# Pooling adds cut into pieces of 256 columns, and the low half of q subtracted on VectorE

## The chip, the cores and the metric

The kernel runs on one core of a Trainium2 chip. The metric is the device time of one launch in microseconds. A core has five engines that each work through a queue of their own in order: TensorE (PE in the profile; PEld are its weight loads), VectorE (DVE), ScalarE (ACT), GpSimd (POOL) and SyncE (SP, which here only issues DMAs). They wait for one another through semaphores.

## The reference

An attention over pooled keys, and then a layer of experts of which each row visits one:

```python
# q (4, 12288, 128), kv (4, 384, 32, 128), w_sr (128, 128)
kv_pool = kv.reshape(B, H // 4, 4, W // 4, 4, C).mean(axis=(2, 4))   # 96 x 8 = 768 keys a batch
k = v = kv_pool.reshape(B, -1, C) @ w_sr
a = softmax(q @ k.T / sqrt(C));  x = a @ v                           # 49152 rows of 128
# experts: E = 8, w1 (8, 128, 1024), w2 (8, 1024, 128)
do_compute = x @ w_skip > 0
e_idx = argmax(x @ w_gate);  gate_w = its softmax probability
y = gate_w * (relu(x @ w1[e_idx]) @ w2[e_idx])
out = where(do_compute, x + y, x)
```

## The kernel before

The program has two stages. The first, up to about 1180 us of the profile, does the attention and the routing; the second runs the experts in a loop over groups of rows. Both changes are in the first.

**Tiles and steps.** The first stage is a loop over `t`, one step for each tile of 128 query rows: 96 tiles a batch, four batches, 384 tiles, and `tb` is the tile's number in its batch. Twelve tiles make a row of work (`RT`), four make a group (`GT`). The order of the instructions is written out by hand (`manual_schedule`): each engine's queue holds its instructions in the order in which the program issues them. A step issues, for different tiles, in this order:

- `scores(t)` on TensorE: six matmuls of q with k. q and k are each held as a high and a low part, so that one product takes three matmuls (L578, L579, L580); the last uses q's low part.
- `attend(t - 6)` and `p_transpose(t - 1)` on TensorE (L641, L616).
- `row_max(t)` on VectorE (L586), once per tile, and `row_exp(t)` on ScalarE (L591), which waits for it. There are two PSUM buffers for scores, so that `scores(t + 2)` waits for `row_exp(t)`.
- `early_a` on ScalarE: q's high part for a later group (`q_hi`, L566). `early_g`: q's low part, `q_lo` = q - `q_hi` (L567), for 512 columns, once every four steps, in the steps that leave 2 when divided by 4. `q_split` puts both there for the group that is used six tiles later.
- `split_v` (L624), `early_v` (L649, L651) and `p_lo(t - 1)` (L599) on VectorE. L599 reads two operands from SBUF; L624 reads one from PSUM and one from SBUF. `p_lo` then issues the DMA that transposes the probabilities (on the SP queue).
- `load_q` and `load_kv`: DMA loads on the SP queue.
- `run_jobs`: the routing of finished rows, a generator that is advanced step by step. Its element operations are on VectorE and GpSimd (L688 to L770). At its end it scatters the 12 tiles of a row to their experts' lists with 12 indirect DMAs, which GpSimd issues (`scatter_rows`, L184), two per step in the steps that leave 6 to 11 when divided by 12. The next row's first routing operations (L692 to L708) come behind the first two of them, and L721 behind the tenth.
- the pooling of the next batch's keys and values: `pool_kv(b + 1, k)` for six chunks k. A chunk is a tile `kvt` of 128 partitions and 16 x 128 columns; GpSimd halves it by adds of 1024, 512 and 256 columns in place (L437), and a last add of 128 columns writes `pooled` (L439). Chunk k's loads are spread over the steps before; four steps after the last one it is put on the list `pools`, and in the next step with `tb % 12 == 11` all four adds of one chunk are issued at once. The first batch's chunks are pooled before the loop, mostly on VectorE; from `tb` = 84 on the pooled chunks are transposed and multiplied for the next batch.

Batches two, three and four are pooled during the loop, so 18 chunks are; the last 96 tiles pool nothing.

Of the kernel before, what the change touches and what calls it, by code (L numbers as in the profile page):

```python
# [9 lines left out]
F32 = mybir.dt.float32  # L10
# [5 lines left out]
ALU = mybir.AluOpType  # L16
# [4 lines left out]
RT = 12  # L21
# [3 lines left out]
def kernel(  # L25
# [11 lines left out]
    nc = tc.nc  # L37
    NR, C, RT, P = q.shape
# [7 lines left out]
    E, _, FF = w1.shape  # L46
# [22 lines left out]
    PSL = 11  # L69
# [97 lines left out]
    op = ctx.enter_context(tc.tile_pool(name="op", bufs=2))  # L167
# [199 lines left out]
    with ExitStack() as p1:  # L367
# [40 lines left out]
        def load_kv(b, k, rs=range(R)):  # L408
            if rs[0] == 0:
                KVT[b, k] = kvp.tile([P, R, R * C], F32, name="kvt")  # L410
            src = kv[b, k * HG * R:(k + 1) * HG * R].rearrange("(i r) (g w) c -> r i g (w c)", r=R, w=R)
            for r in rs:
                nc.sync.dma_start(KVT[b, k][:, r, :], src[r])

        def pooled_out(b, k):
            if k == 0:
                pooled[b] = kprep.tile([P, KC, C], F32, name="pooled")
            return KVT.pop((b, k)), pooled[b][:, k, :]
# [12 lines left out]
        def pool_kv(b, k):  # L431
            t, o = pooled_out(b, k)
            f = t.rearrange("p r x -> p (r x)")
            n = R * R * C
            while n > 2 * C:
                n //= 2
                nc.gpsimd.tensor_tensor(out=f[:, 0:n], in0=f[:, 0:n], in1=f[:, n:2 * n], op=ALU.add)  # L437
                yield
            nc.gpsimd.tensor_tensor(out=o, in0=f[:, 0:C], in1=f[:, C:2 * C], op=ALU.add)  # L439

        HK = NK // 2
# [95 lines left out]
        def prep_kv(b):  # L537
            for f in (kv_transpose, k_matmul):
                for h in range(2):
                    f(b, h * HC, (h + 1) * HC)  # L540
                    yield
            yield from prep_v(b)
# [6 lines left out]
        def load_q(g):  # L549
            r, o = divmod(g, RG)  # L550
            q_sb[g] = qp.tile([P, GW], F32, name="q_sb")
            nc.sync.dma_start(q_sb[g], q[r][:, o * GT:(o + 1) * GT, :].rearrange("c t p -> c (t p)"))

        early_a, early_g, late_a, early_v, jobs = [], [], [], [], []
# [3 lines left out]
        def run_late(q):  # L558
            while q:
                q.pop(0)()  # L560

        def q_split(g):
            q_g = q_sb.pop(g)
            hi = qt.tile([P, GW], F32R, name="q_hi")
            lo = qt.tile([P, GW], F32R, name="q_lo")
            early_a.append(lambda: nc.scalar.copy(hi, q_g))  # L566
            early_g.append(lambda: nc.gpsimd.tensor_tensor(out=lo, in0=q_g, in1=hi.bitcast(F32), op=ALU.subtract))  # L567
            qT[g] = (hi, lo)

        def scores(t):  # L570
            g, j = divmod(t, GT)
            k_hi, k_lo = KV[t // TPB][0:2]
            q_hi, q_lo = (x[:, j * P:(j + 1) * P] for x in qT[g])
            s = ps_s.tile([P, 2, 512], F32, name="s_ps")
            S_PS[t] = s
            for h in range(2):
                sl = slice(h * HK, (h + 1) * HK)
                nc.tensor.matmul(s[:, h, :HK], q_hi, k_hi[:, sl], start=True, stop=False)  # L578
                nc.tensor.matmul(s[:, h, :HK], q_hi, k_lo[:, sl], start=False, stop=False)  # L579
                nc.tensor.matmul(s[:, h, :HK], q_lo, k_hi[:, sl], start=False, stop=True)  # L580
# [3 lines left out]
        def row_max(t):  # L584
            NM[t] = small.tile([P, 1], F32, name="nm")
            nc.vector.tensor_reduce(out=NM[t], in_=S_PS[t][:, :, :HK], axis=AX.XY, op=ALU.max, negate=True)  # L586

        def row_exp(t):
            g, j = divmod(t, GT)
            P_SB[t] = pp.tile([P, 2, HK], F32, name="p_sb")  # L590
            nc.scalar.activation(out=P_SB[t], in_=S_PS.pop(t)[:, :, :HK], func=AF.Exp, bias=NM.pop(t))  # L591

        def p_hi(t):
            P16[t] = hl.tile([P, 2, KD * P], F16, name="p16")
            nc.scalar.activation(out=P16[t][:, 0, :], in_=p_flat(t)[:, 0:KD * P], func=AF.Copy, scale=2.0 ** PEXP)  # L595

        def p_lo(t):
            p16 = P16.pop(t)
            nc.vector.scalar_tensor_tensor(out=p16[:, 1, :], in0=p_flat(t)[:, 0:KD * P], scalar=2.0 ** PEXP,  # L599
                                           in1=p16[:, 0, :], op0=ALU.mult, op1=ALU.subtract)  # L600
            P_SB.pop(t)
            PT[t] = ptp.tile([P, 2 * KD, P], F16, name="pt")
            nc.sync.dma_start_transpose(PT[t], p16.rearrange("p a x -> p (a x)"))

        def p_flat(t):
            return P_SB[t].rearrange("p h x -> p (h x)")
# [3 lines left out]
        def p_transpose(t):  # L610
            g, j = divmod(t, PP)
            if j == 0:
                PTP[g] = acc_ps()
            p = p_flat(t)
            for i in range(KP):
                nc.tensor.transpose(PTP[g][:, (j * KP + i) * P:(j * KP + i + 1) * P],  # L616
                                    p[:, (KD + i) * P:(KD + i + 1) * P], ident)
            if j < PP - 1:
                return
            ps = PTP[g][:, 0:PP * KP * P]  # L620
            hl_t = ptq.tile([P, 2, PP * KP * P], F16, name="ptq")
            PTQ[g] = hl_t.rearrange("p a (j k x) -> p a j k x", j=PP, x=P)
            next_a.append(lambda: nc.scalar.activation(out=hl_t[:, 0, :], in_=ps, func=AF.Copy, scale=2.0 ** PEXP))
            next_v.append(lambda: nc.vector.scalar_tensor_tensor(  # L624
                out=hl_t[:, 1, :], in0=ps, scalar=2.0 ** PEXP, in1=hl_t[:, 0, :], op0=ALU.mult, op1=ALU.subtract))
# [268 lines left out]
        pools = []  # L894
# [14 lines left out]
        while t < NTILE + LAG - 1 or jobs:  # L909
            t += 1  # L910
            b, tb = divmod(t, TPB)
            live = t < NTILE
            for now, nxt in ((split_a, next_a), (split_v, next_v), (late_a, next_l)):
                now.extend(nxt)
                nxt.clear()
            if live:
                scores(t)
            if 0 <= t - LAG < NTILE:
                attend(t - LAG)
            if 0 <= t - 1 < NTILE:  # L920
                p_transpose(t - 1)
            if live:
                row_max(t)
            run_late(early_a)
            run_late(split_a)
            if 0 <= t - 1 < NTILE:
                p_hi(t - 1)
            run_late(late_a)
            if live:
                row_exp(t)  # L930
            run_late(early_g)
            run_late(split_v)
            run_late(early_v)
            if 0 <= t - 1 < NTILE:
                p_lo(t - 1)
            if live:
                if t % GT == 0 and t // GT + RG < NGRP:
                    load_q(t // GT + RG)
                if b + 1 < B:
                    for k, r in KV_T.get(tb, ()):  # L940
                        load_kv(b + 1, k, [r])
                if b + 1 < B and tb == PREP_T:
                    preps.append(prep_kv(b + 1))
                if t in PAD_T:
                    write_pads(*PADS.pop(0))
            first_step(NTILE - t)
            if t == NTILE:
                p_s.close()
                p_kv.close()
                alloc_h(p1.enter_context(tc.tile_pool(name="hp1", bufs=1)))  # L950
                ps_up = p1.enter_context(tc.tile_pool(name="ps_up", bufs=4, space=PSUM))
                alloc["h"] = lambda: ps_up.tile([P, ST], F32, name="up_ps")
            ph = t % GT
            if ph == 1 and t // GT + 2 < NGRP:
                q_split(t // GT + 2)
            ranked = run_jobs(ph)
            if preps and not ranked and (ph in (0, 3) or tb < LAG):
                if next(preps[0], "end") == "end":
                    preps.pop(0)
            if live and b + 1 < B:  # L960
                for k, r in KV_T.get(tb - 4, ()):
                    if r == R - 1:
                        pools.append(pool_kv(b + 1, k))
                if pools and tb % RT == PSL:
                    for _ in pools.pop(0):
                        pass
            for _ in range(2 * (t >= NTILE)):
                next(first)
        for _ in make_table():
# [76 lines left out]
```

## Time and profile before

| | |
|---|---|
| time, median of 3 runs | 2067.53 us (2058.41, 2067.53, 2076.75) |
| profiled execution, its own time | 2057.81 us |
| its span, first to last instruction | 2056.1 us |
| mean granted TensorE clock | 0.949 |
| busy: TensorE, weight loads | 1830.2, 1308.1 us |
| busy: VectorE, ScalarE, GpSimd | 1549.2, 1302.8, 1068.9 us |
| L567 (`q_lo`) on GpSimd | 96 times, 125.9 us |
| L184 scatters of routed rows on GpSimd | 384 times, 385.5 us |
| L586 (`row_max`) on VectorE | 384 times, 363.7 us |

The profile is of one execution. In lines of a timeline the columns are start and duration in us, engine, line, operation, output and inputs with shapes, and in brackets how long the engine stood idle before and what ended that. In lines of groups, after the count: busy us, mean ns of one, idle us before. In lines of stretches: the stretch, its length, each engine's busy us with its number of instructions, then the granted share of the TensorE clock, the busy share of the DMA engines, and GB/s.

### The profile page before, as it was taken

The numbers are of one execution on the slowest core, as the hardware profiler recorded it, in microseconds if no ns is written. First come the engines' busy times: TensorE is split into PE (matmuls) and PEld (weight loads), VectorE is DVE, ScalarE is ACT, GpSimd is POOL, SyncE is SP. The second block draws the span as 40 slices with busy tenths as digits, with TensorE's granted clock in tenths as the row PEclk, the third lists the DMA queues.
The fourth block names the chain that finished last, engine by engine and source line by source line (L and its number), as shares of the span: only waits on it lengthen the run. The fifth ranks groups of instructions, "written<-read, shape, count | busy, mean of one in ns | idle before, by whom it ended". The sixth has DMA issues, their size and how long they took to land. (4 is left out here: it accounts for less than half of the span.)

```text
span 2056.1 us, 42524 instructions
## 1 busy us (share of the span) xinstructions
PE 1830.2 (89%) x13955; PEld 1308.1 (64%) x13955; DVE 1549.2 (75%) x3222; ACT 1302.8 (63%) x2480; POOL 1068.9 (52%) x1296
## 2 busy tenths in 40 slices
PE   4998888989898888898988867999999999999997
PEld 3987878878787787887878733444444444444443
DVE  7987857878686787776867746777777777777776
ACT  3876767767676676766767724656565655555564
POOL 2277674677756768655565753343333333333433
PEclk9999988999999899988999978999999999999999
DMA  7998988889789789878997832433333343333333
GB/s 173 209 193 173 184 165 165 182 157 167 147 161 170 156 177 184 169 164 175 191 185 169 176 73 74 107 98 88 92 88 92 88 103 100 94 90 90 91 89 88
DMA packets 620914, 284.61 MB, mean 138 GB/s; under 512 B 502112, under 2 KB 570848, under 8 KB 620768
## 3 DMA queue, kind: packets, MB, share of 16 engines
q1 hardware_dynamic: 599264, 244.30, 58.3%
q0 software_dynamic: 21504, 38.43, 6.2%
q8 instruction: 83, 1.36, 0.3%
q14 instruction: 63, 0.52, 0.1%
HBM read 90.60 MB, written 78.64 MB: 82 GB/s over the span
## 5 line engine op out<-in xcount | busy, mean ns | idle before, releaser
L184 POOL DMA_INDIRECT out_dram<-o,xin x288 | 299.7, 1040 | 510.7 <-DVE o L293 422.9
L586 DVE TENSOR_REDUCE nm<-s_ps 128x1 f32<-128x768 f32 x384 | 363.7, 947 | 208.7 <-PE s_ps L580 129.8
L270 DVE SCALAR_TENSOR_TENSOR h_lo<-h_ps,h_hi 128x512 f16<-128x512 f32 x544 | 343.1, 685 | 174.1 <-ACT h_hi L269 174.1
L591 ACT ACTIVATE p_sb<-s_ps,nm 128x768 f32<-128x768 f32 x384 | 346.5, 902 | 195.2 <-DVE nm L586 152.9
L184 POOL DMA_INDIRECT scr<-rows,di x384 | 385.5, 1004 | 149.6 <-issue 122.9
L641 PE MATMUL acc_ps<-v_hi,pt 128*128 128x138 f16 x3072 | 339.9, 232 | 90.8 <-DVE ptq L624 36.1
L641 PEld LDWEIGHTS <-pt 128*128 128x128 f16 x4608 | 294.2, 101 | 166.1 <-issue 164.9
L269 ACT ACTIVATE h_hi<-h_ps 128x512 f16<-128x512 f32 x544 | 298.9, 594 | 41.8 <-PE h_ps L268 17.9
L599 DVE SCALAR_TENSOR_TENSOR p<-p_sb,p 128x512 f16<-128x512 f32 x384 | 316.2, 824 | 1.6 <-ACT p L595 1.0
L578 PE MATMUL s_ps<-k_hi,q_hi 128*128 128x384 f32 x768 | 305.1, 397 | 7.6 <-issue 7.6
L641 PE MATMUL acc_ps<-v_lo,pt 128*128 128x138 f16 x1536 | 309.7, 231 | 2.2 <-issue 2.2
L579 PE MATMUL s_ps<-k_lo,q_hi 128*128 128x384 f32 x768 | 268.7, 350 | 4.9 <-issue 4.9
L580 PE MATMUL s_ps<-k_hi,q_lo 128*128 128x384 f32 x768 | 267.6, 348 | 5.7 <-issue 5.7
L595 ACT ACTIVATE p<-p_sb 128x512 f16<-128x512 f32 x384 | 242.0, 630 | 5.5 <-DMA pt<-p 2.2
L266 PE MATMUL h_ps<-xT,w_hi 128*128 128x512 f16 x544 | 206.1, 379 | 24.9 <-issue 24.9
L285 ACT ACTIVATE yT<-y_ps,y_sc 128x512 f32<-128x512 f32 x68 | 46.7, 687 | 276.9 <-PE y_ps L282 217.1
L282 PE MATMUL y_ps<-h_hi,w_hi 128*128 128x512 f16 x544 | 206.2, 379 | 0.0
L282 PE MATMUL y_ps<-h_hi,w_lo 128*128 128x512 f16 x544 | 206.2, 379 | 0.0
L268 PE MATMUL h_ps<-xT,w_lo 128*128 128x512 f16 x544 | 206.1, 379 | 0.0
L267 PE MATMUL h_ps<-xT,w_hi 128*128 128x512 f16 x544 | 206.1, 379 | 0.0
L282 PEld LDWEIGHTS <-w_hi 128*128 128x128 f16 x1152 | 113.4, 98 | 134.7 <-issue 4.5
L567 POOL TENSOR_TENSOR q_lo<-q_sb,q_hi 128x512 fp32r<-128x512 f32 x96 | 125.9, 1312 | 138.0 <-ACT q_hi L566 137.7
(215 smaller groups left out, 3283.7 us busy)
## 6 DMA issues: line engine op xcount, KB each, us to landing
kvt<-in_kv_dram SPq DMA_DIRECT2D x96, 256.0 KB
q_sb<-in_q_dram SPq DMA_DIRECT2D x96, 256.0 KB
out_dram<-rows SPq DMA_DIRECT2D x96, 256.0 KB
xin<-scr SPq DMA_DIRECT2D x75, 264.0 KB, 2.7
w_raw<-in_moe_w_dram SPq DMA_DIRECT2D x38, 512.0 KB, 4.0
scr<-pad SPq DMA_DIRECT2D x32, 264.0 KB
pt<-p SPq DMA_TRANSPOSE x384
scr<-rows,di POOLq DMA_INDIRECT x384
```

The lines of the kernel that those rows point to most:

```text
L184: ins = nc.gpsimd.indirect_dma_start(out=dst, out_offset=bass.IndirectOffsetOnAxis(ap=ids, axis=0), in_=src, in_offset=None, bounds_check= ...
L269: nc.scalar.activation(out=h["hi"][:, c, :], in_=ps, func=AF.Relu)
L270: nc.vector.scalar_tensor_tensor(out=h["lo"][:, c, :], in0=ps, scalar=0.0, in1=h["hi"][:, c, :], op0=ALU.max, op1=ALU.subtract)
L282: nc.tensor.matmul(ps, w[:, c, :], h[x][:, c, :], start=(i == 0), stop=(i == len(terms) - 1))
L578: nc.tensor.matmul(s[:, h, :HK], q_hi, k_hi[:, sl], start=True, stop=False)
L579: nc.tensor.matmul(s[:, h, :HK], q_hi, k_lo[:, sl], start=False, stop=False)
L580: nc.tensor.matmul(s[:, h, :HK], q_lo, k_hi[:, sl], start=False, stop=True)
L586: nc.vector.tensor_reduce(out=NM[t], in_=S_PS[t][:, :, :HK], axis=AX.XY, op=ALU.max, negate=True)
L591: nc.scalar.activation(out=P_SB[t], in_=S_PS.pop(t)[:, :, :HK], func=AF.Exp, bias=NM.pop(t))
L595: nc.scalar.activation(out=P16[t][:, 0, :], in_=p_flat(t)[:, 0:KD * P], func=AF.Copy, scale=2.0 ** PEXP)
L599: nc.vector.scalar_tensor_tensor(out=p16[:, 1, :], in0=p_flat(t)[:, 0:KD * P], scalar=2.0 ** PEXP, in1=p16[:, 0, :], op0=ALU.mult, op1=ALU ...
L641: nc.tensor.matmul(ps[:, j % 2, :], w, v[a][:, k, :], start=(i == 0), stop=(i == len(AVL) - 1))
```

## The change

The subtraction that makes `q_lo` is issued on VectorE in place of GpSimd, and its place in the step moves from behind `row_exp` to behind `p_lo`. The two start-up groups' `q_lo` move to VectorE too.

The pooling's adds of 1024, 512 and 256 columns become four, two and one adds of 256 columns; the last add stays. A step issues one of the eight adds of the chunk at the head of the list (two from `tb` = 74 on), from the step in which the chunk is put on the list, in place of all of them in one step of twelve. Chunks are put on the list at `tb` = 13, 26, 39, 52, 65 and 78.

```diff
             n = R * R * C
+            m = 2 * C
             while n > 2 * C:
                 n //= 2
-                nc.gpsimd.tensor_tensor(out=f[:, 0:n], in0=f[:, 0:n], in1=f[:, n:2 * n], op=ALU.add)
-                yield
+                for c in range(0, n, m):
+                    nc.gpsimd.tensor_tensor(out=f[:, c:c + m], in0=f[:, c:c + m], in1=f[:, n + c:n + c + m], op=ALU.add)
+                    yield
             nc.gpsimd.tensor_tensor(out=o, in0=f[:, 0:C], in1=f[:, C:2 * C], op=ALU.add)
...
-            early_g.append(lambda: nc.gpsimd.tensor_tensor(out=lo, in0=q_g, in1=hi.bitcast(F32), op=ALU.subtract))
+            early_g.append(lambda: nc.vector.tensor_tensor(out=lo, in0=q_g, in1=hi.bitcast(F32), op=ALU.subtract))
...
             if live:
                 row_exp(t)
-            run_late(early_g)
             run_late(split_v)
             run_late(early_v)
             if 0 <= t - 1 < NTILE:
                 p_lo(t - 1)
+            run_late(early_g)
...
-                if pools and tb % RT == PSL:
-                    for _ in pools.pop(0):
-                        pass
+                for _ in range(2 if tb >= 74 else 1):
+                    if pools and next(pools[0], "end") == "end":
+                        pools.pop(0)
```

## The prediction

> **What bounds the kernel now.** I read the busy shares first, then the busy time in chosen stretches, then the count of row maxima (L586, one per query tile) as a clock of tiles, and last the timelines of GpSimd and VectorE.
>
> ```profile
> span 2056.1 us, 42524 instructions
> PE 1830.2 (89%) x13955; PEld 1308.1 (64%) x13955; DVE 1549.2 (75%) x3222; ACT 1302.8 (63%) x2480; POOL 1068.9 (52%) x1296
> ```
>
> No engine is full over the span, so stages decide. The change lives in the attention stage, up to about 1180 us.
>
> ```profile
> core 0: us, PE busy (x) PEld busy (x) DVE busy (x) ACT busy (x) POOL busy (x), PEclk, DMA share, GB/s
> 47.00:117.00 70.00, 69.67 (x762) 65.00 (x763) 64.61 (x116) 61.52 (x113) 25.34 (x34) 1.00 1.04 198
> 354.00:373.00 19.00, 19.00 (x211) 17.71 (x209) 17.78 (x37) 16.50 (x31) 9.62 (x17) 1.00 1.11 192
> 341.00:345.00 4.00, 1.48 (x9) 1.28 (x9) 0.00 (x0) 0.00 (x0) 3.39 (x4) 0.94 1.17 288
> 345.00:352.00 7.00, 5.99 (x38) 5.25 (x38) 4.48 (x8) 4.39 (x8) 5.10 (x6) 0.54 0.38 85
> 770.00:790.00 20.00, 18.13 (x203) 16.63 (x202) 16.31 (x28) 15.96 (x31) 15.17 (x17) 1.00 0.99 215
> ```
>
> In a smooth stretch (354 to 373) TensorE is busy all 19.00 us and VectorE 17.78: TensorE sets the pace and VectorE has 6% left. At 341 to 345 all but GpSimd stand still: VectorE 0.00, TensorE 1.48 of 4; then the granted clock is 0.54 for 7 us. The row maxima give the price:
>
> ```profile
> L586 DVE TENSOR_REDUCE nm<-s_ps x25: 944/952/958, 46.9 to 103.5; 128x1 f32<-128x768 f32 x25
> L586 DVE TENSOR_REDUCE nm<-s_ps x73: 894/949/958, 361.3 to 576.0; 128x1 f32<-128x768 f32 x73
> L586 DVE TENSOR_REDUCE nm<-s_ps x49: 894/957/959, 945.3 to 1087.5; 128x1 f32<-128x768 f32 x49
> L586 DVE TENSOR_REDUCE nm<-s_ps x13: 895/949/958, 760.7 to 792.8; 128x1 f32<-128x768 f32 x13
> ```
>
> Per 12 tiles: 56.6/24 x 12 = 28.3 us before scatters begin, 214.7/72 x 12 = 35.8 with scatters and pooling, 142.2/48 x 12 = 35.5 with scatters and none of the pooling (the last batch), and one odd dozen of 32.1. So pooling itself costs about 0.3 us per dozen tiles, and what comes with the scatters about 7.2. GpSimd around one such place:
>
> ```profile
> 331.39 1.08 POOL L184 DMA_INDIRECT scr<-rows,di  x1 [1.00 <-POOL rows L772]
> 332.78 0.97 POOL L184 DMA_INDIRECT scr<-rows,di  x1 [0.30 <-issue]
> 333.77 0.37 POOL L692 TENSOR_TENSOR d<-lg,mx 128x96 f32<-128x96 f32 x1
> ...
> 336.62 1.07 POOL L184 DMA_INDIRECT scr<-rows,di  x1 [0.52 <-issue]
> 337.99 0.97 POOL L184 DMA_INDIRECT scr<-rows,di  x1 [0.30 <-issue]
> ...
> 343.09 0.97 POOL L184 DMA_INDIRECT scr<-rows,di  x1 [0.30 <-issue]
> 344.06 1.30 POOL L567 TENSOR_TENSOR q_lo<-q_sb,q_hi 128x512 fp32r<-128x512 f32 x1
> 345.53 0.99 POOL L184 DMA_INDIRECT scr<-rows,di  x1 [0.17 <-issue]
> ...
> 347.81 0.62 POOL L721 TENSOR_TENSOR oh_all<-oh,act 128x96 bf16<-128x96 f32 x1
> ...
> 349.93 0.97 POOL L184 DMA_INDIRECT scr<-rows,di  x1 [0.30 <-issue]
> ```
>
> ```profile
> 339.59 0.26 DVE L720 TENSOR_TENSOR oh<-em,mn 128x96 f32<-128x96 f32 x1
> 345.43 0.96 DVE L586 TENSOR_REDUCE nm<-s_ps 128x1 f32<-128x768 f32 x1 [5.59 <-remote]
> ```
>
> Call the 12 scatters of a row s1 to s12. s1 and s2 come in the step whose number leaves 6 when divided by 12 (step 6 below), then two per step to step 11. GpSimd runs behind, so s3 to s8 go out back to back, 1.28 us apart, from 336.62; four scatters in, TensorE stalls, and VectorE waits 5.59 us. q_lo stands behind s8 by program order. Nothing in the trace names what the stalled TensorE lacks; that it comes with scatters in a row is what I use.
>
> **Part 1: q_lo to VectorE.** Prices of like work there, and what an add of 256 columns takes on GpSimd:
>
> ```profile
> L624 DVE SCALAR_TENSOR_TENSOR ptq<-acc_ps,ptq 128x512 f16<-128x512 f32 x140 | 95.2, 680 | 0.0
> L526 DVE TENSOR_TENSOR v_lo<-misc,v_hi 128x411 f16<-128x411 f32 x6 | 3.5, 586 | 2.9 <-ACT v_hi L525 2.9
> L599 DVE SCALAR_TENSOR_TENSOR p<-p_sb,p 128x512 f16<-128x512 f32 x384 | 316.2, 824 | 1.6 <-ACT p L595 1.0
> L567 POOL TENSOR_TENSOR q_lo<-q_sb,q_hi 128x512 fp32r<-128x512 f32 x96 | 125.9, 1312 | 138.0 <-ACT q_hi L566 137.7
> L437 POOL TENSOR_TENSOR kvt<-kvt 128x256 f32<-128x256 f32 x19 | 17.8, 936 | 1.5
> ```
>
> A 512-column subtraction on VectorE is not shown. It lies between 0.59 (411 columns) and the 0.82 mean of L599, the like operation that shares its time with GpSimd; I take 0.68, from L624, of the same width. 96 of them are +65 us of VectorE. GpSimd loses 96 x 1.31, none of it on the path.
>
> Two stand in the start-up, between the k_lo of 31.44 and the k_lo that waits 1.72 us for ScalarE, and are hidden if they take under that:
>
> ```profile
> 31.44 0.41 DVE L465 SCALAR_TENSOR_TENSOR k_lo<-acc_ps,k_hi 128x256 fp32r<-128x256 f32 x1
> 33.57 0.29 DVE L465 SCALAR_TENSOR_TENSOR k_lo<-acc_ps,k_hi 128x128 fp32r<-128x128 f32 x1 [1.72 <-ACT k_hi L464]
> ```
>
> The rest come in steps 2, 6 and 10. About 30 stand in step 10 and lie in the 5.59 us wait; if that wait goes they cost what the others do. Some 64 fall in stretches where VectorE has 1.22 us left in 19 (about 8 tiles, two q_lo, 1.36 us): it goes from 94% to full. Against that, q_lo on GpSimd no longer blocks L599:
>
> ```profile
> 499.29 1.28 POOL L567 TENSOR_TENSOR q_lo<-q_sb,q_hi 128x512 fp32r<-128x512 f32 x1
> 499.92 1.20 DVE L599 SCALAR_TENSOR_TENSOR p<-p_sb,p 128x512 f16<-128x512 f32 x1
> 502.08 0.68 DVE L599 SCALAR_TENSOR_TENSOR p<-p_sb,p 128x512 f16<-128x512 f32 x1
> ...
> 162.75 5.22 POOL L437 TENSOR_TENSOR kvt<-kvt 128x1024 f32<-128x1024 f32 x3
> ...
> 163.70 2.00 DVE L599 SCALAR_TENSOR_TENSOR p<-p_sb,p 128x512 f16<-128x512 f32 x1
> ```
>
> L599 takes 0.68 alone and 1.20 where it starts under q_lo: up to 0.52 in this pair. Not every q_lo meets one; I take 0.2. So VectorE gains 0.48 per q_lo against 0.6 spare; since the spare time isn't where the work falls, I charge 0.2 us each on the path: 64 x 0.2 = **+13 us**, with bounds of 64 x -0.2 = -13 and 64 x 0.68 = +44. The new wait is VectorE's for q_hi, which ScalarE makes first in the same step, ahead of the p_hi that p_lo needs anyway; behind it stand only the routing's small operations and the next row maximum. q_lo comes after p_lo, so the transpose that p_lo issues on the SP queue isn't late. No DMA is moved. TensorE reads q_lo six tiles later, so its lateness costs nothing.
>
> [...]
>
> **Part 2: pooling in pieces.** 18 chunks are pooled in the loop. Before: 5.22 us of adds in one go after s12, plus a last add; L599 at 163.70 lost 1.32 to it. After: seven adds of 256 columns and the last one. The mean of that width is 0.94; the quoted run did 1024 + 512 + 256 columns in 5.22, which is 0.75 per 256, and I take that. Each can hold L599 for at most its own length, though seven are spread over tiles without slack. The dozens with and without pooling differ by 0.3 us, which is all there is to win: 18 x 0.3 = **-5 us**, bounds -18 x 1.32 = -24 and +18 x 0.75 = +14 (one full block per chunk more). Pieces wait for data that was issued four steps earlier; a late one would hold scatters behind it, which nothing waits for at once.
>
> **Part 3: what both do to the scatters**, which I think decides. A chunk's pieces now start in step 13, 26, 39, 52, 65 or 78 of a batch (1, 2, 3, 4, 5 or 6 modulo 12), one per step, two per step for the last chunk. So in every pooled dozen GpSimd's program puts an add behind s4 and s6, and in most behind s8: the row of six becomes pairs with pauses. Rows 0 to 29 scatter in steps 12r + 30 to 12r + 35; five such dozens of the first batch and six each of the second and third hold a pooled chunk: 17 of 30. The nearest row is the odd dozen, where one pause of 2.04 fell into the row:
>
> ```profile
> 771.40 1.07 POOL L184 DMA_INDIRECT scr<-rows,di  x1 [0.53 <-issue]
> 774.52 0.97 POOL L184 DMA_INDIRECT scr<-rows,di  x1 [2.04 <-issue]
> ```
>
> ```profile
> 780.23 0.96 DVE L586 TENSOR_REDUCE nm<-s_ps 128x1 f32<-128x768 f32 x1 [1.89 <-PE s_ps L580]
> ```
>
> There VectorE waited 1.89, the clock stayed at 1.00 (770 to 790, above), and the dozen took 32.1 for 35.8: 3.7 less. Three pauses of 0.75 add to the same, but each is short: I take -3.0; bounds 0 and -7.2. 17 x 3.0 = **-51 us**.
>
> The other 13 dozens lose the pause that q_lo made behind s8: ten scatters in a row instead of six. The stall could last two scatters longer, 2 x 1.28 = 2.6, or not at all, if the stall after 345.53 is only moved forward; I take the middle: 13 x 1.3 = **+17 us**, bounds 0 and +33.
>
> [...]
>
> **Sum**: 13 - 5 - 51 + 17 = -26 us on a profiled execution of 2057.8 (2056.1 of span and 1.7 around it), 2032. The median shown is 2067.5, 9.7 above it; forecast against the median: 2067.5 - 26 = **2042**.
>
> **Rivals.** (1) The pauses are too short to matter: GpSimd's 12 scatters take the same 19.5 us in all (331.39 to 350.90), and TensorE loses the same. Then 13 - 5 + 17 = +25 at most, about +8 if the lost q_lo pause costs nothing: 2075. For it: after q_lo's pause of 1.3 us, scatters go on and TensorE recovers slowly (clock 0.54). Against: the odd dozen. (2) **VectorE becomes the bound**: slower. If the tiles between stalls follow VectorE in full, 64 x 0.68 = +44, no relief from the pauses, nothing from pooling: 2111. VectorE is also what comes next where the stall goes. It decides once its 1.22 us in 19 are eaten, and 2 x 0.68 do that; the trace has it at 94%, so it is near. (3) The stall goes altogether in pooled dozens, and the clock stays at 1.00 as from 770 to 790. For it: one pause took two thirds of the wait; against: the pieces' pauses are shorter. 17 x -5.6 (VectorE's wait) = -95, and +13 + 17 - 5: 2067.5 - 70 = 1998. (4) The change doesn't do what it says, if the adds still run together; but program order puts scatters between them. Only where GpSimd is free, in steps 1 to 5, will they bunch.
>
> **How the numbers follow.** Forecast 0.45, own range 2022 to 2060; rival 1 0.20; rival 2 0.23; rival 3 0.12. 1% (20.7 us) is about what a measurement here can tell from no change. Two thirds of the forecast's case lie below 2047: 0.30, and 0.12 of rival 3: faster 0.42. A third of the forecast and rival 1: same 0.35. Rival 2: slower 0.23. The range, 2000 to 2100, covers the forecast and rival 1 and cuts into the outer ones from inside.
>
> **What would show it.** L567 on VectorE near 680 ns x96; L437 only in 256 columns near 0.75; L599's mean falling from 824 ns; single adds between pairs of scatters; in pooled dozens a VectorE wait well under 5.59 and a clock near 1.00, 32 to 33 us per 12 tiles; in the last batch 36 to 37. I am wrong if pooled and unpooled dozens stay alike, or if TensorE shows waits for VectorE's row maxima between stalls.

## The result, and the profile after

The changed kernel takes **2004.9 us** (median of 4 runs, 1998.8 to 2010.6) against 2067.4 before (4 runs, 2058.4 to 2076.8): a ratio of **0.970, 95% interval 0.9645 to 0.9749**. It is 62.5 us faster; some 26 were forecast. The profiled execution went from 2057.8 to 2004.1.

The engines' busy time in the profile after, to be held against 1830.2, 1549.2 and 1068.9 us for TensorE, VectorE and GpSimd before:

```profile
PE 1807.4 (90%) x13955; PEld 1285.1 (64%) x13955; DVE 1593.6 (80%) x3318; ACT 1299.5 (65%) x2480; POOL 966.4 (48%) x1276
```

The row maxima are again the clock of tiles (first and last start in us; the line is L588 now, two further down). Before, for the first three batches with the first maximum of the fourth, for the fourth, and for 60 tiles of the fourth:

```profile
L586 DVE TENSOR_REDUCE nm<-s_ps x289: 892/950/959, 35.2 to 894.8; 128x1 f32<-128x768 f32 x145
L586 DVE TENSOR_REDUCE nm<-s_ps x96: 894/951/959, 894.8 to 1179.5; 128x1 f32<-128x768 f32 x96
L586 DVE TENSOR_REDUCE nm<-s_ps x61: 894/957/959, 910.4 to 1087.5; 128x1 f32<-128x768 f32 x61
```

and after:

```profile
L588 DVE TENSOR_REDUCE nm<-s_ps x289: 886/949/960, 33.8 to 824.1; 128x1 f32<-128x768 f32 x145
L588 DVE TENSOR_REDUCE nm<-s_ps x96: 893/951/959, 824.1 to 1124.3; 128x1 f32<-128x768 f32 x96
L588 DVE TENSOR_REDUCE nm<-s_ps x61: 894/951/959, 839.8 to 1024.0; 128x1 f32<-128x768 f32 x61
```

The three batches during which keys are pooled shrink from 859.6 to 790.3 us (-69.3), the last one, without pooling, grows from 284.7 to 300.2 (+15.5). Together that is the -53.8 between the two profiled executions; what lies ahead of the first maximum and behind the last changed by under 1.5 us. Counted in dozens, with the last few tiles: the 17 with pooling lose 80.0 us in all (4.7 each), the 13 without gain 26.6 (2.0 each), the 29 tiles ahead of the scatters stay as they were (-0.4).

The same 48 tiles of the second batch, all pooled dozens, before and after, as stretches with each engine's busy time (columns as in the prediction's view of stretches):

```profile
398.60:538.70 140.10, 124.33 (x1257) 113.36 (x1255) 108.84 (x209) 100.94 (x185) 104.29 (x128) 0.94 0.86 163
```

```profile
372.50:495.60 123.10, 117.03 (x1267) 107.42 (x1265) 116.39 (x222) 100.50 (x185) 91.56 (x130) 1.00 1.01 187
895.00:899.00 4.00, 2.20 (x16) 1.15 (x13) 0.00 (x0) 0.41 (x1) 3.42 (x4) 0.53 0.35 97
```

140.1 us became 123.1, 30.8 per dozen; the granted clock rose from 0.94 to 1.00. VectorE is busy 116.39 of the 123.10 and TensorE 117.03: both are near full. The last row is the other side: in the last batch TensorE still stalls, busy 2.20 of 4.00 us with VectorE at 0.00, and the clock is at 0.53. GpSimd's queue in a pooled dozen after:

```profile
446.11 1.07 POOL L184 DMA_INDIRECT scr<-rows,di  x1 [0.15 <-issue]
447.48 0.97 POOL L184 DMA_INDIRECT scr<-rows,di  x1 [0.30 <-issue]
448.48 0.74 POOL L439 TENSOR_TENSOR kvt<-kvt 128x256 f32<-128x256 f32 x1
449.38 1.26 POOL L184 DMA_INDIRECT scr<-rows,di  x1 [0.17 <-issue]
450.95 0.97 POOL L184 DMA_INDIRECT scr<-rows,di  x1 [0.30 <-issue]
451.93 0.74 POOL L439 TENSOR_TENSOR kvt<-kvt 128x256 f32<-128x256 f32 x1
```

and in a dozen of the last batch, with two row maxima that follow each other there:

```profile
886.80 1.07 POOL L184 DMA_INDIRECT scr<-rows,di  x1 [0.52 <-issue]
888.18 0.97 POOL L184 DMA_INDIRECT scr<-rows,di  x1 [0.30 <-issue]
...
896.22 0.97 POOL L184 DMA_INDIRECT scr<-rows,di  x1 [0.30 <-issue]
```

```profile
892.86 0.96 DVE L588 TENSOR_REDUCE nm<-s_ps 128x1 f32<-128x768 f32 x1 [2.41 <-PE s_ps L582]
901.49 0.96 DVE L588 TENSOR_REDUCE nm<-s_ps 128x1 f32<-128x768 f32 x1 [0.46 <-remote]
```

Pairs with an add of 0.74 us between them in the first; s3 to s10, from 886.80 to 897.19, with no other work between them in the second, and 8.6 us from one row maximum to the next. The row maxima before, and then the row maxima, the moved and the cut operations after:

```profile
L586 DVE TENSOR_REDUCE nm<-s_ps 128x1 f32<-128x768 f32 x384 | 363.7, 947 | 208.7 <-PE s_ps L580 129.8
```

```profile
L588 DVE TENSOR_REDUCE nm<-s_ps 128x1 f32<-128x768 f32 x384 | 363.4, 946 | 80.7 <-PE s_ps L582 42.8 <-remote 23.1 <-PE acc_ps L643 6.6
L601 DVE SCALAR_TENSOR_TENSOR p<-p_sb,p 128x512 f16<-128x512 f32 x384 | 286.9, 747 | 1.1 <-ACT p L597 0.8 <-issue 0.2
L439 POOL TENSOR_TENSOR kvt<-kvt 128x256 f32<-128x256 f32 x133 | 108.7, 829 | 52.8 <-DMA kvt<-in_kv_dram 51.8
L569 DVE TENSOR_TENSOR q_lo<-q_sb,q_hi x96: 676/684/1528, 30.4 to 1099.6; 128x512 fp32r<-128x512 f32 x96
```

VectorE's idle time ahead of the row maxima fell from 208.7 us to 80.7. The adds of 256 columns (L439) have a mean of 829 ns and a median of 743.

One thing is needed to read what follows: in two of the groups of runs below (f1, f2, f4, e5 and h1, h2) the unchanged kernel before took 1896 us, in all others 2067 to 2081, and a ratio is always against the runs of before in its own group.

### The profile page after: what moved, and what is told of

Read it like the earlier page. It is cut to its first block, busy times and chain, and to the rows that moved or that the text cites. A ratio compares the mean times of both kernels' runs of the same rounds, so it can differ in the third digit from the quotient of the medians.

```text
span 2002.3 us, 42448 instructions
## 1 busy us (share of the span) xinstructions
PE 1807.4 (90%) x13955; PEld 1285.1 (64%) x13955; DVE 1593.6 (80%) x3318; ACT 1299.5 (65%) x2480; POOL 966.4 (48%) x1276
## 3 DMA queue, kind: packets, MB, share of 16 engines
q0 software_dynamic: 21504, 38.43, 6.4%
## 5 line engine op out<-in xcount | busy, mean ns | idle before, releaser
L184 POOL DMA_INDIRECT scr<-rows,di x384 | 404.2, 1053 | 217.3 <-issue 211.6
L588 DVE TENSOR_REDUCE nm<-s_ps 128x1 f32<-128x768 f32 x384 | 363.4, 946 | 80.7 <-PE s_ps L582 42.8
L643 PE MATMUL acc_ps<-v_hi,pt 128*128 128x138 f16 x3072 | 331.7, 228 | 60.4 <-DVE rs L651 22.3
L643 PEld LDWEIGHTS <-pt 128*128 128x128 f16 x4608 | 286.0, 99 | 142.5 <-issue 141.1
L269 ACT ACTIVATE h_hi<-h_ps 128x512 f16<-128x512 f32 x544 | 299.5, 594 | 43.9 <-PE h_ps L268 20.5
L643 PE MATMUL acc_ps<-v_lo,pt 128*128 128x138 f16 x1536 | 302.1, 227 | 4.3 <-issue 4.3
L580 PE MATMUL s_ps<-k_hi,q_hi 128*128 128x384 f32 x768 | 301.0, 392 | 3.0 <-issue 2.8
L601 DVE SCALAR_TENSOR_TENSOR p<-p_sb,p 128x512 f16<-128x512 f32 x384 | 286.9, 747 | 1.1 <-ACT p L597 0.8
L282 PE MATMUL y_ps<-h_lo,w_hi 128*128 128x512 f16 x544 | 195.1, 379 | 0.0
```

Of the source, the lines that this page charges most:

```text
L184: ins = nc.gpsimd.indirect_dma_start(out=dst, out_offset=bass.IndirectOffsetOnAxis(ap=ids, axis=0), in_=src, in_offset=None, bounds_check= ...
L269: nc.scalar.activation(out=h["hi"][:, c, :], in_=ps, func=AF.Relu)
L282: nc.tensor.matmul(ps, w[:, c, :], h[x][:, c, :], start=(i == 0), stop=(i == len(terms) - 1))
L643: nc.tensor.matmul(ps[:, j % 2, :], w, v[a][:, k, :], start=(i == 0), stop=(i == len(AVL) - 1))
```

## The experiments

**Either part alone, and the pieces moved away from the scatters.** My theory was that the pauses decide (A); the rival was that the gain comes from the work itself, shorter adds and fewer reads by GpSimd (B). e1 takes from the change only the pieces, e2 only the move of q_lo:

```diff
  e1: the change, but
-            early_g.append(lambda: nc.vector.tensor_tensor(out=lo, in0=q_g, ...))
+            early_g.append(lambda: nc.gpsimd.tensor_tensor(out=lo, in0=q_g, ...))   # place in the step as before
  e2: before, but
-            early_g.append(lambda: nc.gpsimd.tensor_tensor(out=lo, in0=q_g, ...))
+            early_g.append(lambda: nc.vector.tensor_tensor(out=lo, in0=q_g, ...))   # place in the step as after
  e3: the change, but
-                for _ in range(2 if tb >= 74 else 1):
-                    if pools and next(pools[0], "end") == "end":
-                        pools.pop(0)
+                if pools and tb % RT < 6:
+                    for _ in range(3):
+                        if pools and next(pools[0], "end") == "end":
+                            pools.pop(0)
```

> Pooling in pieces as after, q_lo on GpSimd as before. Theory A (scatters in a row stall TensorE; a pause between pairs prevents it): pooled dozens stay near 30 us, unpooled dozens return from 37.4 to 35.5 since q_lo again stands behind s8; about 1975 us, faster than the changed kernel. Theory B (the gain is VectorE being held up less by GpSimd, L599 from 824 to 747 ns): L599 comes back to about 780 ns and the time lies between the two kernels, 2005 to 2045.

> q_lo on VectorE as after, pooling in one burst as before. Theory A: every dozen with scatters has ten of them in a row, 37.4 us and more; 30 x 1.9 = +57, about 2115 to 2125 us. Theory B: VectorE is held up less, part of the gain is kept: 2030 to 2055.

> The changed kernel with the same pieces, but three per step and only in steps 0 to 5 of a dozen, where no scatters are issued. Theory A: the pooled dozens lose their pauses and go from 30.3 to about 37.4; 17 x 7 = +115, about 2115 us, though L599 keeps its short waits. Theory B: as the changed kernel, 2005 within 15.

Measured: e1 1998.0 us (ratio 0.9578, 0.9524 to 0.9633; 1975 were expected), e2 2123.9 (1.0205, 1.0145 to 1.0265), e3 2130.4 (1.0245, 1.0180 to 1.0309). The 48 tiles of the second batch in e2, and the same tiles in e3:

```profile
413.00:565.00 152.00, 133.23 (x1260) 117.13 (x1258) 113.24 (x221) 100.54 (x186) 88.07 (x117) 0.88 0.76 151
```

```profile
419.30:574.00 154.70, 134.35 (x1258) 118.94 (x1256) 114.42 (x221) 100.64 (x186) 87.61 (x127) 0.88 0.76 149
L601 DVE SCALAR_TENSOR_TENSOR p<-p_sb,p 128x512 f16<-128x512 f32 x384 | 282.0, 734 | 1.4 <-ACT p L597 1.4
```

123.1, 152.0 and 154.7 us for the same tiles. e3 issues the very instructions of the changed kernel on the same engines; only the adds stand in other steps, and each dozen takes 38.7 in place of 30.8. L601 is even shorter in e3 (734 ns for 747), so the holding up of VectorE isn't where the gain lies. A stands, B falls. e3 against e2 says what the pieces are worth without their place: nothing that shows (the intervals overlap). Moving q_lo alone makes the kernel slower, by about what A expects of the lost pause behind s8 (2115 to 2125): 60 tiles of e2's last batch take 187.8 us, from 960.0 to 1147.8, 37.6 per dozen for 35.4 before.

What q_lo on VectorE costs beside the pieces: e1 is faster than the change (0.9578 for 0.9697), and so again when both ran side by side, as g2 and g1:

> The changed kernel, unchanged. Where before takes about 1896: theory A, no stall left to take away, expects what remains of the change: the burst gone and the low half of q off GpSimd, 1860 to 1870 us like f4_fill_short (which differs from it by some sixty memsets of a tenth of a microsecond), ratio 0.98 to 0.985. Theory B (the memset of f4_fill_short took a stall away): 1900 or more, no gain or a loss. Where before takes about 2070: 2005, ratio 0.97.

> The kernel of e1_pieces_only again (pooling in pieces, the low half of q on GpSimd). Where before takes about 1896: f1_fill_q_gpsimd was 43 us above f2_fill_q_vector there, so the pieces beside the low half of q on GpSimd delay that half, and with it TensorE's next tile: 1900 to 1915, ratio 1.00 to 1.01; its dozens with a tile of 7 us at step 11 stay. If the memsets alone made f1_fill_q_gpsimd slow: 1870 to 1880. Where before takes about 2070: about 1995, ratio 0.958.

g1 took 2018.0 (0.9672, 0.9629 to 0.9714), g2 1998.7 (0.9579, 0.9536 to 0.9623), 19 us less. The row maxima of e1 for the 48 tiles of the second batch and for the 60 of the last:

```profile
L588 DVE TENSOR_REDUCE nm<-s_ps x49: 887/950/959, 378.4 to 500.9; 128x1 f32<-128x768 f32 x49
L588 DVE TENSOR_REDUCE nm<-s_ps x61: 895/951/959, 847.4 to 1025.9; 128x1 f32<-128x768 f32 x61
```

122.5 for the pooled tiles, as good as the change's 123.1; 178.5 for the unpooled ones against 184.2, 1.1 less per dozen. On this showing q_lo on VectorE costs little where there are pauses, and most of its price is the lost pause where there are none. (e1 and the change differ in the engine of q_lo and in its place in the step.)

**Every scatter in a step of its own.** e4 is before, with the scatters of rows 0 to 26 issued one per step (and a fourth row buffer):

```diff
-                if j % 2 == 0 and j > 0 and r < LASTR - 1:
+                if j > 0 and (j % 2 == 0 or r < SNAPR) and r < LASTR - 1:
                     yield
```

> The kernel before, but rows 0 to 26 scatter one tile per step over twelve steps in place of two over six (and a fourth buffer for rows, so that no row waits for its scatters). Theory A: 27 dozens without a stall, 28.5 to 30 us each for 35.8, about 1890 us (down to 1880). Theory B: nothing of VectorE's waits for GpSimd changes, 2067 within 15.

1959.1 us (0.9397, 0.9345 to 0.9449): in A's direction, and short of its number. Its last batch, and what breaks a row there:

```profile
L586 DVE TENSOR_REDUCE nm<-s_ps x61: 892/951/959, 827.3 to 982.6; 128x1 f32<-128x768 f32 x61
```

```profile
882.77 1.28 POOL L567 TENSOR_TENSOR q_lo<-q_sb,q_hi 128x512 fp32r<-128x512 f32 x1 [3.75 <-ACT q_hi L566]
```

31.1 us per dozen. The scatters still run together in threes and fours; q_lo stands between these, once at 872.46 and again here, where GpSimd first waits 3.75 us for q_hi. e5, and g6 again, make the same edit to the changed kernel:

> The changed kernel with the scatters of rows 0 to 26 at one a step instead of two (12 steps instead of 6), and four row buffers instead of three, as e4_singles_before did to before (ratio 0.940, dozens of 30.5 to 34 us in the middle of a batch, the longer ones where the pooling burst pushed scatters into the next row). Theory A: with the pooling in pieces no burst is left, all dozens from the first rows on lie at 30 to 31.5: about 1915 to 1935, ratio 0.92 to 0.935. Rival: one scatter a step lies under every tile and delays each, and the pieces beside it run scatters together in threes as in e4_singles_before, dozens stay at 31 to 34, ratio 0.94 to 0.955.

> The kernel of e5_singles_after again: the changed kernel with the scatters of rows 0 to 26 at one a step, and four row buffers. Where before takes about 2075: if spacing all scatters takes the stall away, the 12 dozens without pooling come to 28.7 to 30 us and the others to 30 to 31 as in e5_singles_after, where there was no stall: 1865 to 1890, ratio 0.90 to 0.91. If pieces between singles bunch them as in e4_singles_before (1959, ratio 0.940): 1910 to 1940. Where before takes about 1896: 1865 again.

e5 ran where before takes 1896: 1864.9 us (0.9832, 0.9816 to 0.9849). g6, where the stall occurs: 2039.4 us (0.9817, 0.9766 to 0.9868), slower than the change, against both theories. The row of g6's last batch, and the scatters of one of its rows:

```profile
L588 DVE TENSOR_REDUCE nm<-s_ps x61: 886/951/958, 875.6 to 1061.8; 128x1 f32<-128x768 f32 x61
```

```profile
922.70 1.08 POOL L184 DMA_INDIRECT scr<-rows,di  x1 [0.52 <-issue]
...
934.84 0.98 POOL L184 DMA_INDIRECT scr<-rows,di  x1 [0.30 <-issue]
```

Ten scatters in 13.1 us, about 1.3 apart, though each was issued in another step, and 37.2 us per dozen. The order of a queue is no timetable: ahead of each of the last nine of these GpSimd stands idle for 0.31 us at most, so when it is behind it runs them off together. In e4 it has q_lo, and its wait for ScalarE, in between. That this difference is the reason was read from the two traces; it wasn't tried by itself.

**A pause made of nothing.** In these a memset on GpSimd that nobody reads goes ahead of s3, s5, s7, s9 and s11 in the dozens in which no pooling is pending; `pools` is made visible to the routing. f2 and g3 are the same kernel, so are f4 and g4. f1 is f2 with q_lo on GpSimd, in its place of before.

```diff
+        fill = rowp.tile([P, 512], F32, name="fill", bufs=1)    # 8 columns in f4/g4, 1024 in g5 and h1
...
                     yield
+                if j % 2 == 0 and j > 0 and not pools:
+                    nc.gpsimd.memset(fill, 0.0)
                 scatter_rows(scr, di[:, j:j + 1], ...)
```

> The kernel of f2_fill_q_vector again (the changed kernel with a memset of 128x512 ahead of s3, s5, s7, s9 and s11 where no pooling is pending). Where before takes about 2070, what was asked of it first: a pause of half a microsecond between the pairs takes the stall away in the 12 dozens without pooling (36 to 38 us to 30 to 31.5): 1920 to 1935, 72 to 84 us below the changed kernel; if only the pooling's own adds do it, about 2005. Where before takes about 1896: 1873 again, 5 to 10 us above the changed kernel, the price of the memsets.

> The kernel of f4_fill_short again: the changed kernel with a memset of 128x8 ahead of s3, s5, s7, s9 and s11 in the dozens without pooling. Where before takes about 2075: if the length of the pause decides, the 12 dozens stay near those of the changed kernel, 35.5 to 37.5 us, and the time is 1990 to 2015; if any instruction between the pairs suffices, they are those of g3_fill_q_vector (31.2 to 34.7), 1925 to 1940. Where before takes about 1896: 1864 again.

> As g3_fill_q_vector, with a memset of 128x1024, an estimated 1.0 us (twice the 527 ns of the 128x528 in the profile of before). Where before takes about 2075: if the length of the pause decides, the 12 dozens fall from g3_fill_q_vector's 31.2 to 34.7 us, for pauses of some 0.4 us, to 29.5 to 31.5, 12 x 2 to 3 = 24 to 36 less: 1897 to 1912, ratio 0.91 to 0.92. If what the shorter pause left has another cause, they stay, and the time is 1930 to 1940. Where before takes about 1896: 1875 to 1885, the memsets' own price.

Where before takes 2078 to 2081: g4 2023.5 us (0.9724, 0.9674 to 0.9774), g3 1933.0 (0.9273, 0.9236 to 0.9311), g5 1905.6 (0.9158, 0.9111 to 0.9205). The length of one memset and the 60 tiles of the last batch, for g4, g3 and g5:

```profile
912.18 0.13 POOL L782 MEMSET fill<- 128x8 f32 x1
L591 DVE TENSOR_REDUCE nm<-s_ps x61: 893/951/959, 858.5 to 1046.6; 128x1 f32<-128x768 f32 x61
```

```profile
855.98 0.55 POOL L782 MEMSET fill<- 128x512 f32 x1
L591 DVE TENSOR_REDUCE nm<-s_ps x61: 893/951/959, 811.3 to 977.3; 128x1 f32<-128x768 f32 x61
```

```profile
844.45 0.98 POOL L782 MEMSET fill<- 128x1024 f32 x1
L591 DVE TENSOR_REDUCE nm<-s_ps x61: 893/950/960, 800.1 to 950.3; 128x1 f32<-128x768 f32 x61
```

Per dozen: 36.8 us without a memset (the change), 37.6 with 0.13 us, 33.2 with 0.55, **30.0 with 0.98**. So the pause needs no add and no reading, only length (here the length goes with the number of columns written; the odd dozen of the prediction had a pause without any work): the stall follows the time for which GpSimd is kept from the next pair. With 0.74 us the pooled dozens, 30.0 to 31.1 in the 48 tiles above, fit in. g3's time is the expected one, but its dozens are not down to the 30 to 31.5 expected, and g4 lies 8 us above its range; g5 is within its own. g5 is the fastest version where the stall occurs, 173 us under the before of its group; the change is 63 under its own.

**Bytes or the scatter itself.** f6 is the change with scatters of 8 values a row, and a last stage that reads other rows, so that only its attention stage can be compared:

```diff
-                scatter_rows(scr, di[:, j:j + 1], rows[:, j, 0:ROW], E * CAP - 1, "scr")
+                scatter_rows(scr8, di[:, j:j + 1], rows[:, j, 0:8], E * CAP - 1, "scr")
```

> The changed kernel, but each scatter writes 8 of a row's values (32 bytes in place of 528) to a buffer of its own, and the last stage reads rows of padding in place of the rows routed, so that its writes are dropped: only the time of the attention stage is to be compared, by its dozens of tiles. As many scatters, as many rows of each, at the same places. Where before takes about 2075: if the bytes that a scatter writes stall TensorE, the dozens without pooling fall from 36 to 38 us to 29 to 31; if it is the scatter itself, with the making of its 128 rows' requests, they stay at 36 to 38.

GpSimd's DMA queue in its profile (packets, MB, share), and its last batch:

```profile
q0 software_dynamic: 21504, 1.42, 1.1%
L589 DVE TENSOR_REDUCE nm<-s_ps x61: 893/951/959, 855.3 to 1039.7; 128x1 f32<-128x768 f32 x61
```

36.9 us per dozen, the change's 36.8. The change has 21504 packets and 38.43 MB there (in both kernels the last stage's own scatters are counted too). With as many packets and a small part of the bytes the stall is the same: it isn't the bytes.

**Where the stall doesn't occur.**

> The kernel of e1_pieces_only (pooling in pieces, the low half of q on GpSimd) with one more GpSimd instruction that computes nothing used: a memset of 128x512 ahead of s3, s5, s7, s9 and s11 of a row, in the dozens in which no pooling is pending. A memset of 128x528 took 527 ns in the profile of before, so each pause between pairs is about 0.5 us; it writes one buffer and reads none. Theory A (a row of scatters run together stalls TensorE, and any occupation of GpSimd between the pairs takes the stall away): the 12 dozens without pooling, 34.8 to 36.8 us in the middle of the last batch in e1_pieces_only, come to 30 to 32, like the pooled ones; 12 x 5 to 6 = 60 to 72 us less than e1_pieces_only, a ratio to before of 0.92 to 0.935. Theory B (the gain comes from the work moved, VectorE's copies no longer meeting GpSimd's reads, and not from the pauses): the memset does nothing or costs its own time, the dozens stay at 35 to 37, ratio 0.955 to 0.965. Theory C (a pause must have the length of a piece's add, some 0.75 us, or must read SBUF): dozens between, 33 to 35, ratio 0.94 to 0.955.

> The changed kernel with the same memset of 128x512 on GpSimd ahead of s3, s5, s7, s9 and s11 in the dozens in which no pooling is pending. Theory A: the 12 dozens without pooling, 36.0 to 37.8 us in the changed kernel, come to 30 to 31.5; 12 x 6 to 7 = 72 to 84 less, about 1920 to 1935, a ratio to before of 0.925 to 0.94. With the stalls gone in both, the difference between this kernel and f1_fill_q_gpsimd is the price of the low half of q on VectorE: 0 to 13 us by theory A (64 x 0 to 0.2), 30 or more if the changed kernel's VectorE is the bound once the stall is gone. Theory B: dozens stay at 36 to 38, ratio 0.965 to 0.975.

> As f2_fill_q_vector, but the memset is of 128x8, the shortest that GpSimd has here, an estimated 0.05 to 0.15 us. If the length of the pause decides (theory A), the dozens without pooling stay close to those of the changed kernel, 35 to 37.5 us, ratio 0.96 to 0.975. If any instruction between the pairs breaks the row up, whatever its length, they come to 30 to 31.5, and the ratio is that of f2_fill_q_vector.

Before took 1896.3 here. f1 1916.1 us (1.0108, 1.0088 to 1.0127), f2 1873.3 (0.9878, 0.9857 to 0.9900), f4 1863.7 (0.9828, 0.9812 to 0.9845). The last batch of f2 and of f4:

```profile
L591 DVE TENSOR_REDUCE nm<-s_ps x61: 894/951/958, 780.9 to 924.7; 128x1 f32<-128x768 f32 x61
```

```profile
L591 DVE TENSOR_REDUCE nm<-s_ps x61: 896/951/959, 779.2 to 922.9; 128x1 f32<-128x768 f32 x61
```

28.8 and 28.7 us per dozen, with scatters run together (f4) or not. That is close to the 28.3 of a dozen without scatters, so these runs can't tell theories A, B and C apart; g3 and g4, the same kernels, did: B falls with g3, A's "any occupation" with g4, and what C says of the length is left. The change itself wasn't run here; f4, which differs from it by memsets of 0.13 us, is 1.7% below before, so, as far as f4 stands for it, the change gains less where there is no stall to take away. They tell something else: f1 and f2 differ only in q_lo's engine and its place in the step, and f2 is 42.8 us **faster**. What waited, in total, times and longest, in the attention stage of f1 and then of f2:

```profile
DVE nm L591 <- PE s_ps L585: 66.7, 98, 5.2
PE misc L753 <- POOL oh_all L726: 29.4, 17, 4.1
```

```profile
DVE nm L591 <- PE s_ps L585: 26.2, 51, 1.8
PE misc L753 <- POOL oh_all L726: 8.9, 4, 2.3
```

With q_lo, pieces and memsets all in GpSimd's queue, `oh_all`, which stands behind the tenth scatter, comes late, and TensorE's counting matmul waits for it. In f1 GpSimd itself also waits for `q_hi` ahead of q_lo, 46.6 us in 18 times, and holds up all that stands behind. The waits for `oh_all` differ by 20.5 us, about half of the 42.8; where the rest lies is open. So GpSimd isn't off the path here: the forecast wrote "none of it on the path" of the 1.31 us it lost per q_lo. The last two kernels were to price this with long pauses in place of the stall, h2 being before with a memset of 1024 columns in every row:

> g5_fill_long (memset of 128x1024 between the pairs where no pooling is pending: 1905.6 us, ratio 0.9158) with the low half of q back on GpSimd. If the forecast's 13 us for that half on VectorE are right, this kernel is the faster by about that: 1885 to 1897, ratio 0.907 to 0.913. If, with the stall gone, the half on GpSimd stands in a queue that the scatters, memsets and pieces fill, and comes late for the tile that needs it (f1_fill_q_gpsimd was 43 us slower than f2_fill_q_vector on the other chip, with tiles of 7 us at step 11): 1930 to 1955, ratio 0.928 to 0.94.

> The kernel before with a memset of 128x1024 ahead of s3, s5, s7, s9 and s11 of every row, pooling in its burst and the low half of q on GpSimd. If pauses between the pairs are all that the pieces bring, its 29 dozens with scatters lose 4 to 6 us each, 2078 - 29 x 4 to 6 = 1904 to 1962, ratio 0.916 to 0.944, no slower than the changed kernel; if the stall needs the pooling spread, or the added memsets push the row's last scatters under the burst and the half of q behind them, it stays above 1990, ratio 0.957 or more.

Before took 1896.3 here too, so the comparison with g5 that h1 was made for isn't to be had: h1 1937.0 (1.0217, 1.0200 to 1.0235), h2 1985.2 (1.0469, 1.0451 to 1.0487). What can be read is that where there is no stall a longer pause only costs: f4 to f2 9.6 us, f1 to h1 20.9. In h1's attention stage TensorE's wait for `oh_all` is longer still, 47.3 us in 24 times.

**Before again**, for its profile:

> The kernel before, unchanged, for a profile on the chip that the other kernels of this call run on. In the second set of runs before took 1896 us, in the first 2081, and the traces of the second set show no tile of 6 to 9 us. Theory A (TensorE's stall under a row of scatters appears on one chip and not on the other; the rest of the kernel is alike): where this kernel takes about 1896, its dozens of tiles hold no tile above 5 us in the scatters' steps 5 to 8, those without pooling take 29 to 30 us, and the ones with the pooling burst 30 to 33, the burst holding the scatters and the low half of q up; where it takes about 2070, the picture is that of the profile before, 34.5 to 37.7. Theory B (the stall is there on both chips and something else differs): tiles of 6 to 9 us in both.

It ran where before takes 2080.7 and took 2080.0, with 36.7 us per dozen in 48 tiles of the second batch (404.5 to 551.2) and 35.4 in 60 of the last (926.1 to 1102.9), for 35.0 and 35.4 in the profile before. So there is no profile of before itself from where it takes 1896.

## Why the prediction was wrong

**The mechanism was right**: the stall comes with scatters run together, pieces between pairs take it away in pooled dozens, and dozens without pooling get worse. e3, g3, g4 and g5 show it. Most of the forecast's own signs came: q_lo on VectorE at 684 ns in the middle, L601 down from 824 to 747 ns, single adds between pairs, a clock of 1.00, the last batch at 36.8 us per dozen ("36 to 37"). The one that didn't is the size: 30.8 us per pooled dozen in the 48 tiles, for "32 to 33".

**The step that failed is the -3.0 us per pooled dozen of Part 3.** The nearest row was the odd dozen, where one pause of 2.04 us was worth 3.7; I cut this to 3.0 because "each is short". With the smaller terms (-0.3 for pooling, two q_lo at 0.2) the forecast for a pooled dozen was -2.9 net; 4.7 were measured, 80 us in 17 in place of 49; if the smaller terms hold, the -3.0 should have been -4.8. The 31 between them are more than the whole error of the sum, 2032 forecast for the profiled execution and 2004 found; the unpooled dozens take back 4.5. The prediction scaled one measured pause down by its length; the runs show that pauses of 0.74 us between the pairs leave little of the stall (with memsets of 0.13, 0.55 and 0.98 us the dozens of the last batch take 37.6, 33.2 and 30.0 us, against 28.7 where there is no stall). That several short pauses do this because the row never becomes dense is my reading. What came is close to rival 3, which had 1998, from -5.6 per pooled dozen, and a chance of 0.12; "the pieces' pauses are shorter" was the argument against it. The median moved by 9 us more than the profiled execution, since before's lay 9.7 below its median.

**The unpooled dozens**: +1.3, or 1.7 with q_lo; measured 2.0. About right, and so is where it comes from (e2), though with some luck, as 1.3 was only the middle of its bounds.

**q_lo on VectorE, +13**: this step's sign isn't supported. Between e1 and the change little of it is left in pooled dozens (122.5 and 123.1 us), and where the stall is absent the move gains, -42.8 us beside memsets, outside the bounds of -13 to +44; without memsets it wasn't tried there. The bounds were drawn from VectorE's time alone.

**Pooling in pieces, -5**: no gain apart from the pauses could be seen (e3 against e2). Adds still lengthen `p_lo` here: in the change's trace L601 takes 1.29 us from 451.94, beside the add of 0.74 us that starts at 451.93, for a median of 0.69. In f1, `p_lo` beside an add and beside a memset:

```profile
508.41 0.93 DVE L604 SCALAR_TENSOR_TENSOR p<-p_sb,p 128x512 f16<-128x512 f32 x1
508.70 1.23 POOL L442 TENSOR_TENSOR kvt<-kvt 128x256 f32<-128x256 f32 x1
...
511.62 0.53 POOL L782 MEMSET fill<- 128x512 f32 x1
511.67 0.69 DVE L604 SCALAR_TENSOR_TENSOR p<-p_sb,p 128x512 f16<-128x512 f32 x1
```

L604 (`p_lo`) takes 0.93 us beside the add, which reads and writes, and 0.69 beside the memset, which only writes. That is one place of each.

**The clock**: before, 0.94 was granted from 341 to 345, where TensorE is busy 1.48 of 4.00 us with gaps of 1.18 and 1.03 us at the longest, and 0.54 in the 7 us behind. In the change's last batch 0.53 goes with 2.20 of 4.00 us busy (895 to 899). What lowers the clock was not shown.

**Rivals.** 1, pauses too short: refuted by the change itself with e3, and by g3 and g5; true only of 0.13 us. 2, VectorE as the bound: it is at 95% in the pooled tiles now, but e1, without q_lo on VectorE, takes as long for them. 4, adds run together: no.

## What to carry to other kernels

Here a stall under a dense row of DMA issues went almost entirely with 0.7 to 1 us of other work between the pairs of issues (30.8 us per dozen tiles with 0.74, 30.0 with 0.98, 28.3 ahead of the scatters): test a dose (no, short, long filler) before arguing how much a pause is worth. Put that work into the queue itself; spreading the issues over steps didn't help in g6, where the engine stands idle for 0.31 us at most between them (37.2 us per dozen). And price a moved operation on the engine that it leaves as well: what is queued behind it may be on the path (TensorE waits 29.4 us for `oh_all` in f1, 8.9 in f2).

## What the runs showed of the hardware

The stall isn't a fixed property of the kernel. g4 and f4 are one kernel: 2023.5 and 1863.7 us, 37.6 and 28.7 per dozen of the last batch, with scatters about as close in both. Before itself takes 2067 to 2081 or 1896. What differs between the two conditions is open. Some expectations above speak of two chips, but the record gives chip number 1 to e1 to e4 (before 2081) and to the f and h runs and e5 (before 1896), and number 5 to the g runs and f6 (before 2078 to 2081): if a number always means the same chip, the chip isn't what differs. What the stalled TensorE lacks stays open too; the bytes that the scatters write are not the cause (f6: 1.42 MB for 38.43, and 36.9 us per dozen for 36.8). The stall in the trace of before says a little more:

```profile
342.48 0.22 PE L641 MATMUL acc_ps<-v_hi,ptq 128*128 128x138 f16 x1 [1.18 <-issue]
342.60 0.27 PE L616 MATMUL acc_ps<-ident,p_sb 128*128 128x128 f32 x1
343.90 0.27 PE L616 MATMUL acc_ps<-ident,p_sb 128*128 128x128 f32 x1 [1.03 <-issue]
```

The last two are the two transposes of one tile `p_sb`. The first had its operand, and the second still starts 1.30 us later, with no semaphore that the profile shows to wait for; so, as far as the profile shows, TensorE wasn't waiting for another engine's result in this place.
